# Decay inside chunks of 128, running state sums on VectorE, v scaled on ScalarE, output copies in free buffers, and another pace of weights

## The chip, the cores and the metric

The kernel runs on one core of one Trainium2 chip. The metric is the device time of one execution in microseconds (us). TensorE does the matmuls, VectorE, ScalarE and GpSimd the elementwise work, and SyncE (SP) issues all DMAs, in one order.

## What is computed

A retention layer, that is causal attention with a fixed decay per head and no softmax, feeds two networks with one hidden layer each.

```python
# q, k, v: (4, 8, 576, 64) float32; x: 2304 tokens x 512; w_in: 512 x 2048; w_out: 2048 x 512
scores = scale * np.matmul(q, k.transpose(0, 1, 3, 2))
gamma = 1.0 - 2.0 ** (-5.0 - np.arange(H, dtype=np.float32))
rel = pos[:, None] - pos[None, :]
Dmat = np.where(rel >= 0, gamma[:, None, None] ** rel[None, :, :], 0.0)
x = np.matmul(scores * Dmat, v)          # then (token, head * 64) rows
h = x @ w_in                             # first network
x = (np.maximum(h, 0.0) + alpha * np.minimum(h, 0.0)) @ w_out
h = x @ w_in2                            # second network
out = (h * (1.0 / (1.0 + np.exp(-1.702 * h)))) @ w_out2
```

All weights come as float64, and the kernel turns them into float32 itself.

## The kernel before

**Attention.** The work is 16 pairs, each two heads of one batch element (`PAIRS`). A sequence of 576 is cut into four chunks of 128 and a rest of 64. Per pair TensorE computes the scores inside each chunk (`a_scores`, tile `sc`), the state sums k^T v (`a_outer`, tile `st`), and the output from both (`a_values`, tile `av`). The state that chunk c reads is the sum over all earlier chunks; TensorE forms each of the four states from scratch, 1 + 2 + 3 + 4 products for each head. The decay is split into a factor on v (`vtab`) and one on the output (`otab`), both counted over the whole sequence from position 256. GpSimd scales v in place (`a_v`). VectorE masks the scores into SBUF (`a_evac`, tile `r`) and scales the output (`a_out`, into `xs`). ScalarE copies the states (`a_states`). At the start eight matmuls on a 34 KB table spread `otab` over the partitions (tile `tab`). The loop over i is a hand-made software pipeline: in step i TensorE does states and scores of pair i, then the output of pair i - 1; the loads (`ld`: q, k, v, 864 KB; `kn`: k once more, 256 KB) run three pairs ahead. Every engine works in the order in which the program issues.

**Weights.** A weight tile (`raw`, 512 KB, three buffers) is loaded, then one ScalarE operation (`w_abs`) and four on VectorE (`w_float`) make it float32 (`cv`, four buffers); a rounded high part (`w_hi`, ScalarE) and the rest (`w_lo`, a subtraction on VectorE) go into the tile `w`. The sixteen `w` slots serve in the attention as buffers of `ld`, `r` and `xs`. Times of all this are written by hand: `at(t, ...)` files an event, and `run_to(t)` issues what is due. In the first stage t counts pairs, later steps of the networks (`base` is the first). Second-network weights are converted early, stored (`w2_store`) and loaded again late (`w2_load`, two halves in one tile `w2f` in the buffers of `raw`).

**Networks.** Tokens lie in five chunks (512, the last, chunk 4, 256), x and the hidden values are split in two as the weights are, and three products of the parts make one. A step is one chunk and one of 16 blocks of hidden units: 12 matmuls into `h` (`mm1`), the activation, the split into `gs`, and two steps later 12 matmuls into four sums `acc` (`mm2`). `BLOCKS` orders the steps: chunks 0 and 1 first run with half of the hidden units, since the other weights are not there yet; their half sums go out to `pt` and come back as `part`. At the end of a block four copies `o` go out:

```python
o = mp.tile([128, 512], F32, tag="g2", name="o", bufs=3)[:, 0:N]
```

These three buffers serve the negative branch `g2` of the first activation too. A step with 512 tokens is 24 matmuls. The split of `gs` is on VectorE in the first 22 steps and on GpSimd after them.

## Time and profile before

| | |
|---|---|
| median of 3 runs (lowest to highest) | 912.92 us (911.67 to 915.03) |
| the profiled execution | 916.01 us, span of its profile 914.2 us |
| TensorE busy | 885.6 us, 97% of the span |
| VectorE, ScalarE, GpSimd busy | 404.8, 328.6, 189.8 us |
| mean granted clock of TensorE | 0.991 |

The span is what the profiler records from the first to the last instruction, and the execution's own time lies 1.8 us above it. A busy share is a mean over stages with different limits. A row of the timeline merges like instructions and gives start, length, engine, line, operation, tiles, count, and in brackets the idle time ahead of it with what ended it. PEld is TensorE's weight load, which runs beside the matmuls.

### The profile page before, as it was taken

The page shows a single profiled execution, that of the slowest core. Times are in us where ns is not written, and L with a number is a line of the kernel's source. Part 1 is how long each engine was busy: PE and PEld are TensorE (multiplying, and loading weights), DVE is VectorE, ACT ScalarE, POOL GpSimd, SP SyncE. Part 2 cuts the span into 40 slices and gives each one's busy share as a digit, 9 for nine tenths or more (in the row PEclk, how much of TensorE's full clock was granted, in tenths as well). Part 3 has the DMA queues.
Part 4 walks back from the last instruction along what each step waited for, and adds up shares of the span by engine and source line. Part 5 has one row for each costly group of instructions (what it writes and reads, how often), then busy time and mean ns, then how long its engine had stood idle before and what let it go on. Part 6 is the DMA issues. An engine that isn't in the chain of part 4 may idle for free.

```text
span 914.2 us, 13404 instructions
## 1 busy us (share of the span) xinstructions
PE 885.6 (97%) x5408; PEld 746.8 (82%) x5408; DVE 404.8 (44%) x625; ACT 328.6 (36%) x618; POOL 189.8 (21%) x173
## 2 busy tenths in 40 slices
...
GB/s 208 268 253 286 103 253 126 128 116 80 52 53 105 217 204 178 150 132 108 161 177 208 137 25 24 1 70 1 23 1 70 1 24 0 58 6 6 34 14 24
DMA packets 37086, 93.30 MB, mean 102 GB/s; under 512 B 4376, under 2 KB 9112, under 8 KB 37024
## 3 DMA queue, kind: packets, MB, share of 16 engines
...
## 4 chain that ended last, share of the span: by engine, by line
PE 67%; issue 15%; DVE 9%; POOL 4%; DMA 3%; ACT 2%; SPq 0%; POOLq 0%; DVEq 0%; ACTq 0%
PE acc L354 33%; PE h L304 33%; POOL gs L81 2%; DVE cv L115 2%; POOL ld L181 2%; DVE g L319 1%; DVE cv L119 1%; DVE cv L111 1%; DVE cv L108 1%; DVE w L81 1%; DVE gs L81 1%; DMA ld<-in_qkv_dram 1%; DMA pt<-o 1%; POOL r L222 1%; DMA out_dram<-o 1%
## 5 line engine op out<-in xcount | busy, mean ns | idle before, releaser
L354 PE MATMUL acc<-gs,w 128*128 128x512 f32 (+1 forms) x1920 | 426.1, 370 | 12.1 <-ACT o L78 3.7
L304 PE MATMUL h<-x,w 128*128 128x512 f32 (+1 forms) x1920 | 420.1, 368 | 0.7 <-DVE xs L248 0.7
L354 PEld LDWEIGHTS acc<-gs,w 128*128 128x128 f32 x1920 | 336.9, 189 | 78.0 <-POOL gs L81 6.2
L304 PEld LDWEIGHTS h<-x,w 128*128 128x128 f32 x1920 | 336.8, 189 | 61.2 <-DVE xs L248 0.9
L81 POOL TENSOR_TENSOR gs<-g,gs 128x512 fp32r<-128x512 f32 (+1 forms) x137 | 164.2, 1199 | 642.9 <-ACT gs L78 532.8
L324 DVE TENSOR_TENSOR g<-h,g 128x512 f32<-128x512 f32 (+1 forms) x80 | 51.0, 638 | 306.4 <-ACT g L323 306.4
L78 ACT ACTIVATE gs<-g 128x512 fp32r<-128x512 f32 (+1 forms) x160 | 94.2, 589 | 104.0 <-DVE g L319 56.2
L323 ACT ACTIVATE g<-h 128x512 f32<-128x512 f32 (+1 forms) x80 | 44.3, 554 | 218.6 <-PE h L304 218.6
L319 DVE SCALAR_TENSOR_TENSOR g<-g,nalpha_sb,g 128x512 f32<-128x512 f32 (+1 forms) x80 | 56.2, 703 | 113.9 <-ACT g L318 113.9
L317 ACT ACTIVATE g<-h 128x512 f32<-128x512 f32 (+1 forms) x80 | 43.6, 545 | 77.8 <-PE h L304 77.7
L115 DVE SCALAR_TENSOR_TENSOR cv<-raw,cv 128x512 int32<-128x512 int32 x64 | 62.8, 981 | 2.2
L103 ACT ACTIVATE cv<-raw 128x512 f32<-128x512 f32 x64 | 42.5, 666 | 35.4 <-DMA raw<-in_w1i_dram 9.9
L119 DVE SCALAR_TENSOR_TENSOR cv<-raw,cv 128x512 int32<-128x512 int32 x64 | 45.3, 707 | 2.2
L318 ACT ACTIVATE g<-h 128x512 f32<-128x512 f32 (+1 forms) x80 | 43.8, 548 | 2.4 <-DMA x<-o 2.4
L78 ACT ACTIVATE w<-cv 128x512 fp32r<-128x512 f32 x32 | 20.2, 631 | 53.6 <-DVE cv L119 53.6
L81 DVE TENSOR_TENSOR x<-xf,x 128x512 fp32r<-128x512 f32 (+1 forms) x32 | 29.9, 934 | 19.9 <-ACT x L78 19.9
L108 DVE TENSOR_SCALAR cv<-cv 128x512 f32<-128x512 f32 x64 | 31.0, 484 | 2.2 <-ACT cv L103 2.1
L214 DVE TENSOR_TENSOR r<-sc,mask_sb 128x1024 f32<-128x1024 f32 x16 | 19.5, 1220 | 26.5 <-PE sc L186 24.7
L186 PEld LDWEIGHTS st<-ld,kn 128*64 128x64 f32 x640 | 21.3, 144 | 11.9 <-POOL ld L181 11.1
L186 PE MATMUL st<-ld,kn 128*64 128x64 f32 x640 | 23.3, 231 | 7.8 <-POOL ld L181 7.7
L111 DVE TENSOR_SCALAR cv<-cv 128x512 int32<-128x512 int32 x64 | 28.2, 441 | 2.2
L78 ACT ACTIVATE o<-acc 128x512 f32<-128x512 f32 (+1 forms) x20 | 11.1, 555 | 44.5 <-DMA out_dram<-o 14.9
...
## 6 DMA issues: line engine op xcount, KB each, us to landing
ld<-in_qkv_dram SPq DMA_DIRECT2D x15, 864.0 KB, 5.0
...
w<-cv SPq DMA_DIRECT2D x32, 256.0 KB, 2.5
...
kn<-in_kn_dram SPq DMA_DIRECT2D x16, 256.0 KB, 5.7
```

Of the source, the lines that this page charges most:

```text
L78: return nc.scalar.activation(out=out, in_=in_, func=ACTF.Copy)
L81: return eng.tensor_tensor(out=out, in0=a, in1=b.bitcast(F32), op=ALU.subtract)
L115: nc.vector.scalar_tensor_tensor(out=g, in0=raw[:, :, 1], scalar=-(1 << 30), in1=g, op0=ALU.bitwise_and, op1=ALU.bitwise_or,)
L119: nc.vector.scalar_tensor_tensor(out=g, in0=raw[:, :, 0], scalar=29, in1=g, op0=ALU.logical_shift_right, op1=ALU.bitwise_or,)
L186: nc.tensor.matmul(out=out, lhsT=lhsT, rhs=rhs, start=start, stop=stop, skip_group_check=True)
L304: nc.tensor.matmul(out=t, lhsT=w[:, cw, k * 128:k * 128 + 128], rhs=x[:, cx], start=(i == 0), stop=(i == 3 * NK - 1),)
L317: nc.scalar.activation(out=g, in_=t, func=ACTF.Relu)
L318: nc.scalar.activation(out=g2, in_=t, func=ACTF.Relu, scale=-1.0)
L319: nc.vector.scalar_tensor_tensor(out=g, in0=g2, scalar=nalpha_sb[:, m:m + 1], in1=g, op0=ALU.mult, op1=ALU.add)
L323: nc.scalar.activation(out=g, in_=t, func=ACTF.Sigmoid, scale=1.702)
L324: nc.vector.tensor_tensor(out=g, in0=t, in1=g, op=ALU.mult)
L354: nc.tensor.matmul(out=acc[0][d], lhsT=w[:, cw, d * 128:d * 128 + 128], rhs=g[:, cx], start=(j == m0 and i == 0), stop=(j == m1 - 1 and i ...
```

## The change

The decay is counted within each chunk of 128. A chunk's own sum k^T v then stands alone, so `a_outer` issues four products for each head. ScalarE scales the states by the decay of 128 positions while it copies them, and VectorE adds the running sum with three operations of 64 columns (`scalar_tensor_tensor`, line 228 after the change). The table of v shrinks to four columns, and ScalarE scales v with three operations, issued before the step's evacuation, no longer at the step's end. The table of the output comes ready from DRAM, 160 KB for each of the first four pairs, so the eight table matmuls and their copies go. PSUM is dealt out anew: `st` has one buffer for two, `av` three for two. In the attention GpSimd does the subtractions of x (`xa_split`) and of seven weights, of which there were eight. The copies `o` of a half block go into the slot of the sixteenth `w` tile (`os`), the others into the buffers of x that the block has read. The reload of second-network weights uses two tiles. The events have other times, and chunk 2 runs before chunk 4.

```diff
...
 BLOCKS = [(0, c, h * HALF, h * HALF + HALF) for h in range(2) for c in (0, 1)]
-BLOCKS += [(0, c, 0, NM) for c in (4, 2, 3)]
+BLOCKS += [(0, c, 0, NM) for c in (2, 4, 3)]
 BLOCKS += [(1, c, 0, NM) for c in range(5)]
...
 
-    vtab_sb = att.tile([128, NP, 9, 1], F32, name="vtab_sb")
+    vtab_sb = att.tile([128, NP, 4], F32, name="vtab_sb")
     mask_sb = att.tile([128, 1, 1, 192], F32, name="mask_sb")
-    rows_sb = wp.tile([8, NP * 128 + S], F32, tag=f"w{TMP['xs'][-1]}", name="rows_sb")
-    otab_sb = att.tile([128, NP, S], F32, name="otab_sb")
+    otab_sb = att.tile([128, NP, 320], F32, name="otab_sb")
     alpha_sb = const.tile([128, NM], F32, name="alpha_sb")
...
 
-    def w_lo(key):
+    def w_lo(key, eng=nc.vector):
         l, c, m = key
         wt[key] = wt[l, m][:, c]
-        sub(nc.vector, wt[key][:, 1], cvs.pop(key), wt[key][:, 0])
-
-    def w_first(t, key, src, gap):
-        at(t - 3.2 * gap, w_load, key, src, key[2])
+        sub(eng, wt[key][:, 1], cvs.pop(key), wt[key][:, 0])
+
+    def w_first(t, key, src, eng):
+        at(t - 1.5, w_load, key, src, key[2])
         at(t, w_abs, key)
-        at(t + gap, w_float, key)
-        at(t + 2 * gap, w_hi, key)
-        at(t + 3 * gap, w_lo, key)
+        at(t + 0.5, w_float, key)
+        at(t + 1.0, w_hi, key)
+        at(t + 1.5, w_lo, key, eng)
 
...
     def w2_load(m):
-        f = cvp.tile([128, 2, DM], F32, tag="raw", name="w2f", bufs=3)
-        nc.sync.dma_start(out=f, in_=w2s[m])
-        for c in range(2):
-            cvs[2, c, m] = f[:, c]
+        for c, (tag, bufs) in enumerate((("raw", 3), ("cv", 4))):
+            cvs[2, c, m] = cvp.tile([128, DM], F32, tag=tag, name="w2f", bufs=bufs)
+            nc.sync.dma_start(out=cvs[2, c, m], in_=w2s[m][:, c])
 
...
             nc.sync.dma_start(out=t[:, 1152:1728], in_=qkv[b, p, :, 1152:1728])
-            nc.sync.dma_start(out=rows_sb, in_=otab)
         else:
...
         nc.sync.dma_start(out=n, in_=kn[b, p])
+        if i < NP:
+            nc.sync.dma_start(out=otab_sb[:, i], in_=otab[:, i])
         q = [t[:, j * 128:j * 128 + 128] for j in (0, 1, 4, 5)] + [t[:, 768:832]]
...
 
+    def scale(out, in_, by):
+        nc.scalar.activation(out=out, in_=in_, func=ACTF.Copy, scale=by)
+
     def a_v(i):
         v, p = ld[i][2], PAIRS[i][1]
-        nc.gpsimd.tensor_tensor(
-            out=v, in0=v, in1=vtab_sb[:, p].to_broadcast([128, 9, 64]), op=ALU.mult
-        )
+        for e in range(2):
+            scale(v[:, e:8:2], v[:, e:8:2], vtab_sb[:, p, e:e + 1])
+        scale(v[:, 8], v[:, 8], vtab_sb[:, p, 2:3])
 
...
         if i not in s_t:
-            s_t[i] = aps.tile([128, 512], F32, tag="st", name="st", bufs=2)
-        for c in range(1, 5):
-            for j in range(c):
-                for e, o in enumerate(halves):
-                    mm(s_t[i][o, c * 64:c * 64 + 64], n[:, j, o], v[:, 2 * j + e], c == 1 and i > 0, j == c - 1)
+            s_t[i] = aps.tile([128, 512], F32, tag="st", name="st")
+        for j in range(4):
+            for e, o in enumerate(halves):
+                mm(s_t[i][o, j * 64 + 64:j * 64 + 128], n[:, j, o], v[:, 2 * j + e], j == 0 and i > 0, True)
 
...
         if i not in s_t:
-            s_t[i] = aps.tile([128, 512], F32, tag="st", name="st", bufs=2)
+            s_t[i] = aps.tile([128, 512], F32, tag="st", name="st")
         for o in halves:
...
     def a_states(i):
-        copy(r_t[i][1], s_t.pop(i)[:, 0:320])
+        s, g = r_t[i][1], vtab_sb[:, PAIRS[i][1], 3:4]
+        scale(s, s_t.pop(i)[:, 0:320], g)
         nc.gpsimd.tensor_tensor(
-            out=r_t[i][1][:, 0:64], in0=r_t[i][1][:, 0:64], in1=mask_sb[:, 0, 0, 128:192], op=ALU.mult
-        )
+            out=s[:, 0:64], in0=s[:, 0:64], in1=mask_sb[:, 0, 0, 128:192], op=ALU.mult
+        )
+        for c in range(128, 320, 64):
+            nc.vector.scalar_tensor_tensor(
+                out=s[:, c:c + 64], in0=s[:, c - 64:c], scalar=g, in1=s[:, c:c + 64],
+                op0=ALU.mult, op1=ALU.add,
+            )
 
...
         r, s = r_t.pop(i)
-        t = [aps.tile([128, 512], F32, tag=f"av{h}", name="av") for h in range(2)]
+        t = [aps.tile([128, 512], F32, tag="av", name="av", bufs=3) for h in range(2)]
         av_t[i] = t
...
             nc.vector.tensor_tensor(
-                out=xs[:, s0:s1], in0=t[h][:, 0:s1 - s0], in1=otab_sb[:, p, s0:s1], op=ALU.mult
+                out=xs[:, s0:s1], in0=t[h][:, 0:s1 - s0], in1=otab_sb[:, p, 0:s1 - s0], op=ALU.mult
             )
...
         copy(x[:, 0], f)
-        sub(nc.vector, x[:, 1], f, x[:, 0])
+        sub(nc.gpsimd, x[:, 1], f, x[:, 0])
 
...
         if layer == 0:
-            g2 = mp.tile([128, 512], F32, tag="g2", name="g2", bufs=3)[:, 0:N]
+            g2 = mp.tile([128, 512], F32, tag="g2", name="g2", bufs=2)[:, 0:N]
             nc.scalar.activation(out=g, in_=t, func=ACTF.Relu)
...
         if m == m1 - 1:
+            if m1 < NM:
+                os = wp.tile([128, NK, 512], F32, tag=f"w{NM - 1}", name="os")
             for d in range(NK):
-                o = mp.tile([128, 512], F32, tag="g2", name="o", bufs=3)[:, 0:N]
+                if m1 < NM:
+                    o = os[:, d]
+                else:
+                    o = homes[layer, c].tile([128, 512], F32, tag=f"x{d}", name="o")[:, 0:N]
                 if m0:
...
         src = (w1i, w1o)[key[1]]
-        if n < 8:
-            w_first(3 + 1.6 * n, key, src, 0.25)
+        if n < 7:
+            t = 2.5 + 1.8 * n
         elif n < 16:
-            w_first(base - 1 + 0.68 * (n - 8), key, src, 0.5)
+            t = base - 1.2 + 0.66 * (n - 7)
         else:
-            w_first(base + 5 + 0.85 * (n - 16), key, src, 0.5)
+            t = base + 5.5 + 0.95 * (n - 16)
+        w_first(t, key, src, nc.gpsimd if n < 7 else nc.vector)
     for i in range(n_a):
...
         nc.vector.memset(wz, 0.0)
-        wps = aps.tile([128, 512], F32, tag="av0", name="wps")
+        wps = aps.tile([128, 512], F32, tag="av", name="wps", bufs=3)
         for i in range(8):
...
                 a_outer(i)
+            if i + 1 < n_a:
+                a_v(i + 1)
             run_to(i)
...
                 a_states(i)
-            if i == 0:
-                for p in range(NP):
-                    for h, (s0, s1) in enumerate(((0, 256), (256, S))):
-                        t = aps.tile([128, 512], F32, tag=f"av{h}", name="tab")[:, 0:s1 - s0]
-                        r0 = NP * 128
-                        mm(t, rows_sb[:, p * 128:p * 128 + 128], rows_sb[:, r0 + s0:r0 + s1], True, True)
-                        copy(otab_sb[:, p, s0:s1], t)
             run_to(i + 0.25)
...
                 a_load(i + 3)
-            if i + 1 < n_a:
-                a_v(i + 1)
             run_to(i + 0.75)
...
             steps += [(layer, c, m, m0, m1) for m in range(m0, m1)]
-        n_x = 2
-        for layer, c, m0, _ in BLOCKS[4:]:
+        homes = {(0, c): xp[c] for c in range(2)}
+        for n, (layer, c, m0, _) in enumerate(BLOCKS[4:]):
+            homes[layer, c] = xp[n % 2]
             for k in range(NK):
-                t = starts[layer, c, m0] - 7 + 1.5 * k
+                t = starts[layer, c, m0] - 6 + 1.3 * k
                 at(t - 2, x_load, layer, c, k)
-                at(t, x_split, layer, c, k, xp[n_x % 2])
-            n_x += 1
+                at(t, x_split, layer, c, k, xp[n % 2])
         for c in range(2):
             for d in range(NK):
-                at(starts[0, c, HALF] + 5 + 0.3 * d, part_load, c, d)
-        t2 = starts[0, 4, 0] + 3
+                at(starts[0, c, HALF] + 7.5, part_load, c, d)
         n1 = starts[1, 0, 0]
...
             for c, src in ((0, w2i), (1, w2o)):
-                key = (2, c, m)
-                t = t2 + 1.25 * (2 * m + c)
+                key, n = (2, c, m), 2 * m + c
+                if n < 5:
+                    t = base + 26.2 + 0.9 * n
+                elif n < 21:
+                    t = base + 33.5 + 0.85 * (n - 5)
+                else:
+                    t = base + 47.5 + 1.45 * (n - 21)
                 at(t - 1.6, w_load, key, src, m)
...
     p = np.arange(128)
-    j = np.stack([p - 256, p - 128, p, p + 128])
-    vt = (gam[:, None, None] ** (-j[None].astype(np.float64))).reshape(NP, 2, 4, 128)
-    tail = (gam[:, None] ** -(256.0 + np.arange(64))).reshape(NP, 1, 128)
-    vt = np.concatenate([vt.transpose(0, 2, 1, 3).reshape(NP, 8, 128), tail], axis=1)
-    d["vtab"] = vt.transpose(2, 0, 1).astype(np.float32)
-    i = np.concatenate([np.arange(256) - 256, np.arange(320)])
-    ot = gam[:, None] ** i[None, :].astype(np.float64) / float(D) ** 0.5
-    rows = np.concatenate([np.repeat(np.eye(H), 64, axis=1), ot], axis=1)
-    d["otab"] = rows.astype(np.float32)
+    decay = lambda n: (gam[:, None] ** n.astype(np.float64)).reshape(NP, 2, -1)
+    half = lambda t: np.repeat(t, 64, axis=1)
+    key = decay(-p)
+    tail = decay(-128 - p[:64]).reshape(NP, 128)
+    vt = np.stack([key[:, 0], key[:, 1], tail, half(decay(np.array([128])))[..., 0]], axis=2)
+    d["vtab"] = vt.transpose(1, 0, 2).astype(np.float32)
+    ot = decay(np.arange(320) % 128) / float(D) ** 0.5
+    d["otab"] = half(ot).transpose(1, 0, 2).astype(np.float32)
     tri = p[None, :] >= p[:, None]
     return {n: np.ascontiguousarray(d[n]) for n in _INS}
```

TensorE's order within one pair (st: states, sc: scores, av: output) was this:

```order
L186 MATMUL st<-ld,kn 64x64 x20
L186 MATMUL sc<-ld 128x128 x8
L186 MATMUL st<-ld 64x64 x2
L186 MATMUL av<-ld,r 64x128 x6
L186 MATMUL av<-ld,r 64x64 x2
```

and is now:

```order
L188 MATMUL st<-ld,kn 64x64 x8
L188 MATMUL sc<-ld 128x128 x8
L188 MATMUL st<-ld 64x64 x2
L188 MATMUL av<-ld,r 64x128 x6
L188 MATMUL av<-ld,r 64x64 x2
```

Only the first row has become shorter; nothing has changed its place. On VectorE, where a pair of the second batch element and a weight conversion meet (xs: output, cv: weight), the order was:

```order
L214 TENSOR_TENSOR r<-sc,mask_sb 128x1024
L108 TENSOR_SCALAR cv<-cv 128x512
L111 TENSOR_SCALAR cv<-cv 128x512
L115 SCALAR_TENSOR_TENSOR cv<-raw,cv 128x512
L119 SCALAR_TENSOR_TENSOR cv<-raw,cv 128x512
L81 TENSOR_TENSOR x<-xs,x 128x448
L248 TENSOR_TENSOR xs<-av,otab_sb 128x256
L248 TENSOR_TENSOR xs<-av,otab_sb 128x320
L81 TENSOR_TENSOR w<-cv,w 128x512
```

and is now:

```order
L215 TENSOR_TENSOR r<-sc,mask_sb 128x1024
L228 SCALAR_TENSOR_TENSOR r<-r,vtab_sb 128x64 x3
L107 TENSOR_SCALAR cv<-cv 128x512
L110 TENSOR_SCALAR cv<-cv 128x512
L114 SCALAR_TENSOR_TENSOR cv<-raw,cv 128x512
L118 SCALAR_TENSOR_TENSOR cv<-raw,cv 128x512
L255 TENSOR_TENSOR xs<-av,otab_sb 128x256
L255 TENSOR_TENSOR xs<-av,otab_sb 128x320
```

The two subtractions are gone, and the three multiply-adds stand behind the evacuation. On ScalarE, at the same place, the order was:

```order
L78 ACTIVATE r<-st 128x320
L103 ACTIVATE cv<-raw 128x512
L78 ACTIVATE x<-xs 128x448
L78 ACTIVATE w<-cv 128x512
L78 ACTIVATE r<-st 128x320
L78 ACTIVATE x<-xs 128x448
```

and is now:

```order
L179 ACTIVATE r<-st,vtab_sb 128x320
L102 ACTIVATE cv<-raw 128x512
L77 ACTIVATE x<-xs 128x448
L179 ACTIVATE ld<-ld,vtab_sb 128x4x64 x2
L179 ACTIVATE ld<-ld,vtab_sb 128x64
L179 ACTIVATE r<-st,vtab_sb 128x320
L77 ACTIVATE w<-cv 128x512
L77 ACTIVATE x<-xs 128x448
```

Three scalings of v (tile `ld`) now stand ahead of each copy of the states (`r<-st`).

## Rows read from the trace of the kernel before

**Rows 1.** Busy time of each engine by stretch, then PEclk (granted clock), DMA share, GB/s.

```profile
23.02:94.79 71.77, 62.91 (x1248) 55.88 (x1248) 54.58 (x87) 19.69 (x40) 21.02 (x26) 0.98 0.76 267
102.82:914.20 811.38, 795.67 (x3840) 669.30 (x3840) 339.47 (x521) 300.95 (x563) 164.20 (x137) 1.00 0.26 85
...
62.00:66.00 4.00, 2.33 (x32) 1.99 (x34) 2.83 (x5) 1.42 (x3) 1.54 (x2) 0.93 0.96 376
66.00:68.40 2.40, 2.40 (x28) 2.28 (x26) 1.92 (x3) 1.15 (x2) 0.00 (x0) 0.50 0.06 24
```

**Rows 2.** Timeline of the attention, TensorE: state matmuls, and the networks' first matmuls.

```profile
16.16 2.40 PE L186 MATMUL st<-ld,kn 128*64 128x64 f32 x40
...
23.02 1.39 PE L186 MATMUL st<-ld,kn 128*64 128x64 f32 x40
...
27.87 1.39 PE L186 MATMUL st<-ld,kn 128*64 128x64 f32 x40 [0.20 <-POOL ld L181]
...
94.79 1.39 PE L186 MATMUL st<-ld,kn 128*64 128x64 f32 x40 [0.19 <-POOL ld L181]
...
102.82 8.46 PE L304 MATMUL h<-x,w 128*128 128x512 f32 x36 [0.67 <-DVE xs L248]
```

**Rows 3.** TensorE's waits after 103 us: total us, times, longest us.

```profile
PE acc L354 <- ACT o L78: 3.7, 3, 2.2
...
PE acc L354 <- DVE o L363: 2.0, 1, 2.0
```

**Rows 4.** Timeline, TensorE and ScalarE, near the end of the first network.

```profile
465.23 2.88 PE L304 MATMUL h<-x,w 128*128 128x512 f32 x12
...
492.97 1.15 ACT L78 ACTIVATE w<-w2f 128x512 fp32r<-128x512 f32 x2 [3.54 <-DMA w2f<-w]
...
501.19 2.88 PE L354 MATMUL acc<-gs,w 128*128 128x512 f32 x12
```

**Rows 5.** Instructions grouped by line and shape: busy us, mean ns, idle before.

```profile
L81 POOL TENSOR_TENSOR gs<-g,gs 128x512 fp32r<-128x512 f32 x106 | 139.7, 1317 | 564.1 <-ACT gs L78 481.9 <-PE acc L354 82.2
...
L319 DVE SCALAR_TENSOR_TENSOR g<-g,nalpha_sb,g 128x512 f32<-128x512 f32 x64 | 48.5, 758 | 100.6 <-ACT g L318 100.6
...
L214 DVE TENSOR_TENSOR r<-sc,mask_sb 128x1024 f32<-128x1024 f32 x16 | 19.5, 1220 | 26.5 <-PE sc L186 24.7 <-PE st L186 1.9
...
L319 DVE SCALAR_TENSOR_TENSOR g<-g,nalpha_sb,g 128x256 f32<-128x256 f32 x16 | 7.7, 480 | 13.3 <-ACT g L318 13.3
...
L78 ACT ACTIVATE r<-st 128x320 f32<-128x320 f32 x16 | 6.9, 433 | 23.7 <-PE st L186 23.6
```

**Rows 6.** Timeline, VectorE: both output products; a conversion's first operation, and its subtraction.

```profile
27.82 0.81 DVE L248 TENSOR_TENSOR xs<-av,otab_sb 128x256 f32<-128x256 f32 x2
...
107.78 0.42 DVE L108 TENSOR_SCALAR cv<-cv 128x512 f32<-128x512 f32 x1
...
110.03 0.68 DVE L81 TENSOR_TENSOR w<-cv,w 128x512 fp32r<-128x512 f32 x1
```

**Rows 7.** Timeline, GpSimd and VectorE at 78 us.

```profile
78.25 1.15 POOL L181 TENSOR_TENSOR ld<-ld,vtab_sb 128x576 f32<-128x576 f32 x1
78.34 1.33 DVE L108 TENSOR_SCALAR cv<-cv 128x512 f32<-128x512 f32 x1
```

**Rows 8.** Timeline, GpSimd: the second pair's v.

```profile
10.61 1.15 POOL L181 TENSOR_TENSOR ld<-ld,vtab_sb 128x576 f32<-128x576 f32 x1 [0.53 <-DMA ld<-in_qkv_dram]
```

**Rows 9.** Timeline, TensorE and ScalarE, at the end of the first half block.

```profile
152.47 2.88 PE L304 MATMUL h<-x,w 128*128 128x512 f32 x12
...
157.40 4.58 PE L354 MATMUL acc<-gs,w 128*128 128x512 f32 x12 [2.04 <-DVE o L367]
...
159.38 0.60 ACT L78 ACTIVATE o<-acc 128x512 f32<-128x512 f32 x1 [4.71 <-DMA pt<-o]
...
161.81 2.91 PE L304 MATMUL h<-x,w 128*128 128x512 f32 x12
```

**Rows 10.** DMA issues: KB each, median us from issue to landing.

```profile
ld<-in_qkv_dram SPq DMA_DIRECT2D x15, 864.0 KB, 5.0
```

4 lines of the change are left out of this document (2 added, 2 removed).

## Prediction

> **What bounds the kernel now.** I read the stretches first: they set TensorE's busy time against the span, stage by stage. From the third pair's state matmuls to the last pair's, 23.02 to 94.79 us, TensorE is busy 62.91 of 71.77 us, and VectorE is busy 54.58 [rows 1]. In the stage of the two networks TensorE is busy 795.67 of 811.38 us [rows 1]. That leaves two things to win: work of TensorE and waits in the first 103 us, and about 16 us of gaps behind it. TensorE's timeline gives the pace of the first stage. A pair that meets little resistance takes 27.87 - 23.02 = 4.85 us, 0.20 of it a wait for GpSimd's scaling of v; the 13 pairs between the third and the last take 71.77 / 13 = 5.52 us each [rows 1, 2]. The pairs that take longer carry a weight conversion on VectorE. The waits of the second stage then say what the gaps are: copies of finished sums (o) that stand still [rows 3], and one stretch around 480 us in which weights of the second network come late [rows 4].
>
> **Attention, TensorE.** A pair's state sums go from 20 matmuls to 8. The profile counts each as two, and 40 of them take 1.39 us [rows 2], so 24 fewer save 0.83 us. The wait of 0.20 us is for v, which ScalarE will scale one step earlier in the order. The floor of a pair becomes 4.85 - 0.20 - 0.83 = 3.82 us.
>
> **Attention, VectorE.** It keeps the evacuation, 1.22 us [rows 5], and the two output products, 0.81 us [rows 6]. It gains three multiply-adds of 64 columns. No row shows these. The same operation takes 758 ns at 512 columns and 480 ns at 256 [rows 5], 1.09 ns a column, which leads to about 270 ns at 64 as my estimate; the bounds are nothing and 480 ns each. I take 0.27, the end of that line, so 0.8 us a pair (0 to 1.44). It loses the subtractions of x and of the attention-time weights to GpSimd. A conversion without its subtraction, four operations, is 110.03 - 107.78 = 2.25 us [rows 6]. Seven of 16 pairs carry one: 1.22 + 0.81 + 0.81 + 2.25 = 5.1 us. The other nine need 2.8 and stand at TensorE's 3.82. If no slack passes from one pair to the next, the mean is (7 x 5.1 + 9 x 3.82) / 16 = 4.4 us; if all of it passes, 3.85. I take 4.4, because before, too, conversions lengthen the pair in which they stand.
>
> **Attention, GpSimd.** Its scaling of v goes; eight subtractions of 448 or 512 columns and seven of weights come, at 1.32 us each [rows 5], 20 us in all (four of 64 columns are small). What one costs VectorE is the open price. A VectorE operation of 0.42 us [rows 6] that began 0.09 us after a GpSimd operation took 1.33, ending 0.27 us behind it [rows 7]. So the bounds are nothing and the whole 20 us (1.24 us a pair). I take a tenth, 0.13 a pair: the evacuation and the output products read PSUM, and the three multiply-adds are short. The Trainium skill (SBUF — State Buffer, "Who interferes with whom") says that a VectorE instruction with two SBUF inputs and a GpSimd instruction that reads SBUF shut each other out for the whole instruction. The rows agree, 1.33 us for 0.42; by that rule the multiply-adds and conversions are exposed to each new subtraction, and all of them meeting one would give the third rival's time. My pace is 4.4 + 0.1 = 4.5 us a pair, between 3.8 and 5.6.
>
> **Attention, the engines that cover.** ScalarE was busy 19.69 us in 13 pairs, 1.5 each [rows 1]. Its three scalings of v cost at most three times the 433 ns of its 320-column copy [rows 5], 1.3 us: 2.8 of 4.5, so I cost them at nothing. What stands behind them matters more: the copy of the states is queued behind the next pair's scaling, which waits for that pair's load. State sums have one PSUM buffer now, so the next pair's state matmuls and the multiply-adds wait for that copy. If this cover fails, the price is the second rival's.
>
> **Attention, start.** The eight table matmuls go; before, the second pair's states began at 16.16 and the third's at 23.02 [rows 2]. The second load came at 10.61 [rows 8]. Ahead of it now lies a table of 160 KB for 34 KB, 0.3 us at 376 GB/s [rows 1]. Add 1.3 for v and 0.43 for the states' copy: the second pair begins near 12.7, 3.4 us earlier. Its states need 24 of 40 matmuls less of the 2.40 us taken there [rows 2], 1.4 more, unless TensorE is granted its high clock later than before. I take 4.1 (3.4 to 4.9). The last stretch, 94.79 to 102.82 [rows 2], I leave: it loses 0.83 of matmuls and gains a conversion ahead of the last product. Sum: 4.1 + 13 x (5.52 - 4.5) = 17.4 us.
>
> **Networks, copies of sums.** At the end of the first half block TensorE needs 161.81 - 152.47 = 9.34 us for two groups that take 5.44 elsewhere (2.72 each): 3.9 us lost, 2.04 as a wait and the rest because the next 12 matmuls take 4.58 us and not 2.88 [rows 9]. The cause stands on ScalarE: its copy into o waits 4.71 us for a store, since three buffers serve o and the negative branch [rows 9]. The other block ends cost 3.7 us in three waits and 2.0 in one [rows 3]. The new buffers (the slot of the sixteenth weight tile, later x's own) have four places each, and their earlier readers are two steps back. So these 3.9 + 3.7 + 2.0 = 9.6 us go; the lower bound is nothing, if the places come free late.
>
> **Networks, pace of weights.** From 465.23 to 501.19 TensorE does 11 groups, 29.9 us of work in 35.96: 6.0 us lost, while ScalarE waits for second-network weights, 3.54 us in one case, ahead of the copy that feeds TensorE [rows 4]. Their reloads share the SP queue and the buffers with the last conversions. Now all conversions are issued before the first reload, so I count 6.0 gained (bounds 0 and 6.0). Against it: nine first-network weights instead of eight fall into the first steps, where VectorE is full; the extra one is 2.25 us and a subtraction of about 0.7, of which I take 0.5 as a stall (0 to 2.9). The order of chunks 2 and 4 moves the short steps away from the early conversions and under the late ones: nothing, plus or minus 1.5. Sum: 9.6 + 6.0 - 0.5 = 15.1 us.
>
> **The sum.** 17.4 + 15.1 = 32.5 us. The profiled execution took 916.0 us (span 914.2), 0.3% above the median of 912.9; from that median, 880.
>
> **Rivals.** *TensorE paces every pair* at 3.82 us: slack does pass on, as VectorE's mean of 3.85 allows. Gain 4.9 + 22.1 + 15.6: 870 us. *Loads pace the pairs*: 1.38 MB a pair with its share of weights at the stretch's 267 GB/s [rows 1] is 5.2 us, and ScalarE stands in front of the states' copy until they land (5.0 us from issue [rows 10]). For it: the loads have less lead now. Against: 376 GB/s was reached at a share of 0.96 [rows 1], 3.7 us a pair. Gain 4.1 + 4.2 + 15.1: 889.5 us. *GpSimd shuts VectorE out*: 5.6 us a pair; gain 4.1 - 1.0 + 15.1: 895 us. *The copies still wait* because the new places are held by stores or readers: without the 9.6, 890 us. *Slower*: TensorE stays at its lower clock, 1.2 GHz, through the attention. From 66.0 to 68.4 us it was granted 0.50, after four microseconds in which it was busy for 2.33 [rows 1]. A pair then takes 7.64 us, 3.14 above my pace; from 32.5 / 3.14 = 10.4 pairs on the kernel is slower, and 13 give 921 us. Sparser matmuls speak for it; that TensorE held a clock of 0.98 over the 13 pairs at 88% busy [rows 1] speaks against, since 3.82 of 4.5 is 85%. The Trainium skill (TensorE: Matmul & The Clock Gate, "Part 1: The HAM clock gate") makes the low state the default and activity what lifts it; the stretch at 66 us agrees.
>
> **How the numbers follow.** My forecast has 0.66 and a range of its own of 868 to 889. TensorE-paced 0.09, loads 0.10, GpSimd 0.08, waiting copies 0.04, slower 0.03. 867 to 893 holds the first, the fast one, the loads and the waiting copies, less the ends. About 0.5%, 4.6 us, is what a measurement can tell from no change. Only the clock ends slower: 0.03. Within 0.5% needs two of the bad cases together: 0.02. Faster: 0.95.
>
> **What would show it.** The stage of the networks begins near 85 us; the state matmuls stand about 4.5 us apart, wider where a conversion stands; the 64-column multiply-adds take near 0.27 us. No wait for o at a block end, and none of ScalarE for w2f near the end of the first network. I would be wrong if ScalarE's scaling waits long for loads, if multiply-adds run to GpSimd's end, or if the granted clock falls in the attention.

## The result, and the profile after

The changed kernel takes 881.41 us, median of 4 runs (880.08 to 883.86), against 913.71 us of the kernel before, also 4 runs: a ratio of 0.965, with an interval of 0.962 to 0.968. The forecast was 880. The profiled execution took 883.86 us, its span 882.1, which is 32.1 below the span of before. The stretches show where these 32.1 us lie.

```profile
19.60:80.70 61.10, 53.26 (x940) 48.02 (x938) 57.19 (x103) 32.22 (x75) 22.96 (x32) 0.94 0.82 297
87.39:882.10 794.71, 790.01 (x3842) 668.89 (x3840) 346.49 (x529) 304.78 (x565) 164.60 (x137) 1.00 0.27 87
```

These answer to the first two of [rows 1]: the 13 pairs between the third and the last, and the networks. VectorE is now busy 57.19 of 61.10 us, so it has taken TensorE's place as the busiest engine of the attention. In the networks all that is left above TensorE's own 790 us is 4.7 us. TensorE's timeline gives the borders:

```profile
13.00 1.12 PE L188 MATMUL st<-ld,kn 128*64 128x64 f32 x16 [2.68 <-ACT r L179]
...
19.60 0.63 PE L188 MATMUL st<-ld,kn 128*64 128x64 f32 x16
...
23.33 0.64 PE L188 MATMUL st<-ld,kn 128*64 128x64 f32 x16
...
80.70 0.63 PE L188 MATMUL st<-ld,kn 128*64 128x64 f32 x16
...
87.39 8.50 PE L311 MATMUL h<-x,w 128*128 128x512 f32 x36
```

Against [rows 1, 2] the start of the third pair gained 23.02 - 19.60 = 3.4 us, the 13 pairs 71.77 - 61.10 = 10.7 (5.52 to 4.70 a pair), the end of the attention 8.03 - 6.69 = 1.3, and the networks 811.38 - 794.71 = 16.7. An unhindered pair takes 23.33 - 19.60 = 3.73 us; the longest of the 13 takes 7.06. Behind the attention TensorE waits for no copy o any more; [rows 3] have become these two:

```profile
PE acc L361 <- ACT gs L77: 1.0, 1, 1.0
PE acc L361 <- POOL gs L80: 0.4, 2, 0.3
```

The new operations, by line and shape (busy us, mean ns, idle before):

```profile
L228 DVE SCALAR_TENSOR_TENSOR r<-r,vtab_sb 128x64 f32<-128x64 f32 x48 | 22.1, 460 | 7.1 <-ACT r L179 5.8
...
L179 ACT ACTIVATE ld<-ld,vtab_sb 128x256 f32<-128x256 f32 x32 | 14.5, 499 | 21.9 <-DMA ld<-in_qkv_dram 21.8
...
L80 POOL TENSOR_TENSOR w<-cv,w 128x512 fp32r<-128x512 f32 x7 | 9.0, 1285 | 1.8 <-ACT w L77 1.8
```

A multiply-add takes 460 ns in the mean, not 270. VectorE's timeline shows both kinds, and GpSimd's what ran beside them:

```profile
39.80 0.92 DVE L228 SCALAR_TENSOR_TENSOR r<-r,vtab_sb 128x64 f32<-128x64 f32 x3
40.63 0.81 DVE L255 TENSOR_TENSOR xs<-av,otab_sb 128x256 f32<-128x256 f32 x2
41.36 1.24 DVE L107 TENSOR_SCALAR cv<-cv 128x512 f32<-128x512 f32 x1
...
45.60 2.58 DVE L228 SCALAR_TENSOR_TENSOR r<-r,vtab_sb 128x64 f32<-128x64 f32 x3
```

```profile
41.19 1.13 POOL L80 TENSOR_TENSOR x<-xs,x 128x448 fp32r<-128x448 f32 x1 [1.20 <-ACT x L77]
...
45.76 1.13 POOL L80 TENSOR_TENSOR x<-xs,x 128x448 fp32r<-128x448 f32 x1 [1.75 <-ACT x L77]
46.84 1.26 POOL L80 TENSOR_TENSOR w<-cv,w 128x512 fp32r<-128x512 f32 x1
```

At 39.80 three multiply-adds take 0.92 us with nothing large on GpSimd. At 45.60 the same three take 2.58 us, beside GpSimd's two subtractions from 45.76 to 48.1. Last, what answers to [rows 10]: a load of q, k and v now lands 7.0 us after its issue, no longer 5.0.

```profile
ld<-in_qkv_dram SPq DMA_DIRECT2D x15, 864.0 KB, 7.0
```

### The profile page after: what moved, and what is told of

It reads as the page before. It is cut to its first block, busy times and chain, and to the rows that moved or that the text cites. A ratio compares the mean times of both kernels' runs of the same rounds, so it can differ in the third digit from the quotient of the medians.

```text
span 882.1 us, 12646 instructions
## 1 busy us (share of the span) xinstructions
PE 863.1 (98%) x5008; PEld 734.4 (83%) x5008; DVE 414.8 (47%) x654; ACT 345.5 (39%) x658; POOL 189.8 (22%) x176
## 4 chain that ended last, share of the span: by engine, by line
PE 86%; DVE 8%; issue 2%; ACT 1%; DMA 1%; POOL 0%; SPq 0%; POOLq 0%; ACTq 0%
PE acc L361 41%; PE h L311 40%; PE av L188 2%; DVE cv L114 1%; DVE r L228 1%; PE sc L188 1%; DVE cv L110 1%; DMA ld<-in_qkv_dram 1%; DVE r L215 1%; PE st L188 1%; DVE cv L107 1%; DVE xs L255 1%; DVE g L326 1%; DVE gs L80 1%; DVE w L80 1%
## 5 line engine op out<-in xcount | busy, mean ns | idle before, releaser
L361 PE MATMUL acc<-gs,w 128*128 128x512 f32 (+1 forms) x1920 | 420.9, 368 | 1.5 <-ACT gs L77 1.0
L114 DVE SCALAR_TENSOR_TENSOR cv<-raw,cv 128x512 int32<-128x512 int32 x64 | 66.7, 1042 | 2.2
L118 DVE SCALAR_TENSOR_TENSOR cv<-raw,cv 128x512 int32<-128x512 int32 x64 | 44.8, 699 | 2.2
L179 ACT ACTIVATE ld<-ld,vtab_sb 128x256 f32<-128x256 f32 (+1 forms) x48 | 18.3, 444 | 21.9 <-DMA ld<-in_qkv_dram 21.8
L228 DVE SCALAR_TENSOR_TENSOR r<-r,vtab_sb 128x64 f32<-128x64 f32 x48 | 22.1, 460 | 7.1 <-ACT r L179 5.8
L188 PE MATMUL av<-ld,r 64*64 64x128 f32 (+1 forms) x256 | 17.9, 273 | 6.5 <-DVE xs L255 6.4
```

The lines of the kernel that those rows point to most:

```text
L114: nc.vector.scalar_tensor_tensor(out=g, in0=raw[:, :, 1], scalar=-(1 << 30), in1=g, op0=ALU.bitwise_and, op1=ALU.bitwise_or,)
L118: nc.vector.scalar_tensor_tensor(out=g, in0=raw[:, :, 0], scalar=29, in1=g, op0=ALU.logical_shift_right, op1=ALU.bitwise_or,)
L188: nc.tensor.matmul(out=out, lhsT=lhsT, rhs=rhs, start=start, stop=stop, skip_group_check=True)
L361: nc.tensor.matmul(out=acc[0][d], lhsT=w[:, cw, d * 128:d * 128 + 128], rhs=g[:, cx], start=(j == m0 and i == 0), stop=(j == m1 - 1 and i ...
```

## Experiments

Each kernel is the changed one with one edit, unless said otherwise. To read them by stage, this table has, from the profiled execution of each, when the networks begin, the mean of the 13 pairs between the third and the last, and the length of the networks. Experiments 1, 2, 7 and 8 shared a chip with runs of before at 915.74 us, 3, 4, 9 and 10 at 915.25, 5, 6 and 11 at 915.33, and 12 at 914.40.

| kernel | median us | ratio to before | networks begin | us a pair | networks |
|---|---|---|---|---|---|
| before | 913.71 | 1 | 102.82 | 5.52 | 811.4 |
| changed | 881.41 | 0.965 (0.962 to 0.968) | 87.39 | 4.70 | 794.7 |
| 1: sums on TensorE | 881.50 | 0.962 (0.957 to 0.967) | 84.70 | 4.59 | 794.2 |
| 2: subtractions on VectorE | 882.97 | 0.964 (0.958 to 0.970) | 85.60 | 4.61 | 795.1 |
| 3: both | 881.68 | 0.963 (0.960 to 0.966) | 86.34 | 4.58 | 794.5 |
| 4: v on GpSimd, late | 894.62 | 0.978 (0.975 to 0.981) | 100.19 | 5.80 | 793.9 |
| 5: v on GpSimd, early | 889.95 | 0.973 (0.968 to 0.978) | 93.19 | 5.21 | 794.1 |
| 6: v on ScalarE, late | 881.65 | 0.964 (0.959 to 0.968) | 86.48 | 4.73 | 793.8 |
| 7: old buffers of o | 883.28 | 0.964 (0.959 to 0.969) | 85.21 | | 796.3 |
| 8: old pace, second network | 889.15 | 0.971 (0.966 to 0.976) | 86.48 | | 800.6 |
| 9: old pace and buffers | 893.92 | 0.976 (0.973 to 0.980) | 84.64 | | 807.8 |
| 10: old pace, new buffers | 890.59 | 0.974 (0.971 to 0.976) | 86.24 | | 802.1 |
| 11: sums added from PSUM | 879.13 | 0.962 (0.956 to 0.968) | 82.01 | 4.34 | 794.6 |
| 12: the same, conversions in halves | 879.47 | 0.962 (0.960 to 0.964) | 83.73 | 4.35 | 794.0 |

The changed kernel and experiments 7 to 10 have the same attention but for a shift in the first weights' times, and their networks begin between 84.64 and 87.39 us. Differences below 3 us in that column are therefore not read as effects. Networks that are those of the changed kernel (experiments 1 to 6, 11 and 12) take 793.8 to 795.1 us, each in one profiled execution, so the last column is good to about 1 us. The medians come from chips on which the kernel before took 0.7 to 2.0 us more than the 913.71 that belong to 881.41; from one chip to another the ratios are the fairer comparison.

**Theories.** The prediction put the attention's gain on fewer state matmuls and on VectorE's lighter load, and that of the networks on new buffers for o (9.6 us) and on the weights' pace (6.0). The rival for the attention: it hangs on the edit that was costed at nothing, v scaled by ScalarE. The rival for the networks: the pace alone removes the waits for o. A further rival for the attention was not run: the weights converted there are seven instead of eight, and they are loaded and converted at other times.

### 1. State sums on TensorE again, without multiply-adds

```diff
-        for j in range(4):
-            for e, o in enumerate(halves):
-                mm(s_t[i][o, j * 64 + 64:j * 64 + 128], n[:, j, o], v[:, 2 * j + e], j == 0 and i > 0, True)
+        for c in range(1, 5):
+            for j in range(c):
+                for e, o in enumerate(halves):
+                    mm(s_t[i][o, c * 64:c * 64 + 64], n[:, j, o], v[:, 2 * j + e], c == 1 and i > 0, j == c - 1)
...
-        for c in range(128, 320, 64):
-            nc.vector.scalar_tensor_tensor(
...
```

> The changed kernel with the state sums on TensorE again: 20 state matmuls a pair instead of eight, and no multiply-adds on VectorE. Left out is the decay between chunks in these sums, so the values differ; the amount of work is that of the kernel before. My theory, TensorE paces the pairs without a conversion and VectorE the others: the pairs of 3.73 us go to about 4.55, the longer ones get shorter by about the multiply-adds, and the networks begin at 90 to 93 us, total 884 to 887 us. Rival, TensorE paces all pairs: 0.83 us on each of 16, networks near 100 us, total near 894. Rival, VectorE paces all: networks near 80 us, total near 873.

Measured: 881.50 us, no slower than the changed kernel; neither the theory's 884 to 887 us nor a rival's time. Its stretch of 13 pairs:

```profile
18.46:78.07 59.61, 58.58 (x1253) 54.08 (x1249) 44.59 (x68) 31.82 (x75) 23.21 (x30) 1.00 0.87 304
```

TensorE is busy 58.58 of 59.61 us, 5.3 more than with the change, and VectorE 12.6 less. TensorE now paces the pairs, where VectorE does in the changed kernel. The load has only changed engines: what TensorE saves by the smaller sums, the multiply-adds take back on VectorE.

### 2. The subtractions back on VectorE

```diff
-        sub(nc.gpsimd, x[:, 1], f, x[:, 0])
+        sub(nc.vector, x[:, 1], f, x[:, 0])
...
-        w_first(t, key, src, nc.gpsimd if n < 7 else nc.vector)
+        w_first(t, key, src, nc.vector)
```

> The changed kernel with the 15 large and four small subtractions of the attention back on VectorE. My theory is that VectorE's own work with the time for which GpSimd holds it sets the pace of the longer pairs: VectorE gets about 11 us of subtractions (12 of x and seven of weights, 0.23 to 0.7 us each) and is freed of about 9 us (48 multiply-adds at 0.46 us on average instead of 0.27). So the networks should begin within 2 us of the 87.4 us of the changed kernel, and the multiply-adds should all take under 0.3 us. Rival, GpSimd's hold alone costs the time: the networks begin 3 us or more earlier, near 84 us. Rival, moving the subtractions was the gain: they begin 5 us or more later.

Measured: 882.97 us and 4.61 us a pair, the same time. The multiply-adds fall to 289 ns in the mean, since GpSimd no longer holds them up, and VectorE spends what it saves so on the subtractions. Moving them neither gains nor loses.

### 3. Both of these undone together

> The changed kernel with both parts undone that made no difference one at a time: 20 state matmuls a pair without multiply-adds (leaves out the decay between chunks), and the subtractions of x and of the attention's weights on VectorE. Theory (the gain of the attention lies elsewhere: tables, time and engine of v, seven conversions at another pace): 881 to 884 us, pairs of 4.6 to 4.8 us. Rival (each of the two alone makes the slack that the pairs need, so only undoing both shows it): pairs of 5.2 us or more, 888 to 892 us.

```profile
20.17:79.70 59.53, 58.78 (x1253) 54.53 (x1249) 49.49 (x85) 32.25 (x76) 4.86 (x12) 1.00 0.85 305
```

```profile
20.17 1.33 PE L188 MATMUL st<-ld,kn 128*64 128x64 f32 x40
...
24.60 1.33 PE L188 MATMUL st<-ld,kn 128*64 128x64 f32 x40
```

Measured: 881.68 us, 4.58 us a pair; the theory held. Here TensorE has the 20 state matmuls of before and VectorE the subtractions of before, and yet the 13 pairs take 59.53 us where before took 71.77 [rows 1]. The gain needs neither of the two edits on which the prediction had built its pace. An unhindered pair takes 24.60 - 20.17 = 4.43 us here and took 4.85 before, with the same matmuls. Of these 0.42 us the trace of before showed 0.20 as a wait for v.

### 4. v scaled by GpSimd at the step's end, as before

```diff
-        for e in range(2):
-            scale(v[:, e:8:2], v[:, e:8:2], vtab_sb[:, p, e:e + 1])
-        scale(v[:, 8], v[:, 8], vtab_sb[:, p, 2:3])
+        by = vtab_sb[:, p, 4:13].rearrange("p (n o) -> p n o", o=1).to_broadcast([128, 9, 64])
+        nc.gpsimd.tensor_tensor(out=v, in0=v, in1=by, op=ALU.mult)
...
-            if i + 1 < n_a:
-                a_v(i + 1)
             run_to(i)
...
                 a_load(i + 3)
+            if i + 1 < n_a:
+                a_v(i + 1)
             run_to(i + 0.75)
```

> The changed kernel with v scaled by GpSimd at the end of the step, as before. Theory (v on ScalarE and issued earlier is a part of the gain in the attention): TensorE's states wait for GpSimd again, the multiply-adds meet one more GpSimd operation a pair; the 13 pairs go from 4.7 to about 5.1 us each, 885 to 888 us. Rival (ScalarE's 21.8 us of waits for loads hold up the copies of the states, so that taking v off ScalarE helps): 4.4 us a pair, 876 to 879 us. Neither matters: 880 to 883 us.

Measured: 894.62 us, 13.2 above the changed kernel (0.978 of before against 0.965) and more than any theory had said; the networks begin at 100.19 us. This one edit takes back 12.8 of the 15.4 us that the attention had gained. GpSimd's timeline, then TensorE's:

```profile
27.82 0.32 POOL L80 TENSOR_TENSOR x<-xs,x 128x64 fp32r<-128x64 f32 x1 [1.44 <-ACT x L77]
28.09 1.17 POOL L184 TENSOR_TENSOR ld<-ld,vtab_sb 128x576 f32<-128x576 f32 x1
```

```profile
29.32 0.69 PE L187 MATMUL st<-ld,kn 128*64 128x64 f32 x16 [2.48 <-POOL ld L184]
```

The scaling of v begins the moment that a 64-column subtraction of x lets it. GpSimd had waited 1.44 us for that subtraction's input, a copy of ScalarE. TensorE's states, queued behind all this, waited 2.48 us, and 18.1 us over 13 pairs. An engine works in the order of issue: v of the next pair stood behind work of this pair that waits for two other engines.

### 5. v scaled by GpSimd, but issued early

The edit of experiment 4 without the move to the step's end.

> The changed kernel with v scaled by GpSimd, but issued where the change issues it, ahead of the step's evacuation. Theory (the place decides: at the step's end the scaling stood behind GpSimd's mask product of the same step, which waits for ScalarE's copy of the states, which waits for TensorE's states, and the next pair's states wait for the scaling, so that a pair lasted as long as this loop): issued early it is outside the loop, pairs of 4.7 to 4.9 us, 881 to 885 us. Rival (the engine decides: one more GpSimd operation a pair, and each shuts VectorE out): pairs of 5.2 us or more, 889 to 895 us, as when it stood at the step's end.

Measured: 889.95 us, 4.7 below experiment 4 and 8.5 above the changed kernel. The rival's range held (889 to 895 us, pairs of 5.2 or more), but the place has its part. Out of the queue's end, v no longer makes TensorE wait; what it does now stands in VectorE's group of multiply-adds and in TensorE's waits, both over the 13 pairs:

```profile
L227 DVE SCALAR_TENSOR_TENSOR r<-r,vtab_sb 128x64 f32<-128x64 f32 x37 | 24.6, 664 | 0.9
```

```profile
PE av L187 <- DVE xs L254: 11.6, 7, 3.1
```

With one more GpSimd operation a pair the multiply-adds of this stretch take 664 ns, where the changed kernel's take 493; VectorE's output products come late, and TensorE waits 11.6 us for them. VectorE is busy 7.8 us more than in the changed kernel, 6.9 of them in the multiply-adds, which the kernel before did not have.

### 6. v scaled by ScalarE, but at the step's end

> The changed kernel with v scaled by ScalarE, but issued at the step's end, as before. Theory of the place: the scaling stands behind the copy of the states and the splits on ScalarE, TensorE's states wait for it, pairs of 5.1 to 5.6 us, 887 to 894 us. Rival (the engine): 880 to 884 us, pairs of 4.7 us.

Measured: 881.65 us. On ScalarE the place costs nothing, so the theory of the place fell for it. TensorE waits 4.2 us for the scaled v, and the pairs are no longer for it. In the changed kernel, then, with the multiply-adds on VectorE and the subtractions on GpSimd, v must not be on GpSimd. What v there costs without these two, as in the kernel before, no run shows.

### 7. Copies o in the three shared buffers again

```diff
-            g2 = mp.tile([128, 512], F32, tag="g2", name="g2", bufs=2)[:, 0:N]
+            g2 = mp.tile([128, 512], F32, tag="g2", name="g2", bufs=3)[:, 0:N]
...
-                if m1 < NM:
-                    o = os[:, d]
-                else:
-                    o = homes[layer, c].tile([128, 512], F32, tag=f"x{d}", name="o")[:, 0:N]
+                o = mp.tile([128, 512], F32, tag="g2", name="o", bufs=3)[:, 0:N]
```

> The changed kernel with the output copies in the three buffers that they share with the negative branch, as before. The term of the prediction: 9.6 us come back, less what the first long step after a half block hides now, so 888 to 891 us, with waits of TensorE for the copies at the two ends of the first half blocks, 2 us each, and the lower granted clock behind the first. Rival, the other pace of weights had taken these waits away by itself: 881 to 883 us.

Measured: 883.28 us; the networks take 796.3 us, 1.6 more, where 7 to 9.6 were expected. In the whole time nothing of it is clear of noise (0.964 of before against 0.965). TensorE waits for o at the end of the first half block alone, 1.0 and 0.3 us.

### 8. The old pace and reload of the second network's weights

```diff
-                if n < 5:
-                    t = base + 26.2 + 0.9 * n
-                elif n < 21:
-                    t = base + 33.5 + 0.85 * (n - 5)
-                else:
-                    t = base + 47.5 + 1.45 * (n - 21)
+                t = base + 35 + 1.25 * n
...
-        for c, (tag, bufs) in enumerate((("raw", 3), ("cv", 4))):
-            cvs[2, c, m] = cvp.tile([128, DM], F32, tag=tag, name="w2f", bufs=bufs)
-            nc.sync.dma_start(out=cvs[2, c, m], in_=w2s[m][:, c])
+        f = cvp.tile([128, 2, DM], F32, tag="raw", name="w2f", bufs=3)
+        nc.sync.dma_start(out=f, in_=w2s[m])
```

> The changed kernel with the conversions of the second network's weights at their times of before (one each 1.25 steps from the 35th step) and the reload in one tile. The term of the prediction: about 6 us come back, 887 us, and ScalarE waits for reloaded weights in front of the copies that feed TensorE, in the last eight steps of the first network. Rival, those waits came with the old order of chunks or from the output copies: 881 to 883 us.

Measured: 889.15 us; the networks take 800.6 us, 5.9 more. TensorE's waits in them:

```profile
PE acc L362 <- ACT gs L77: 4.1, 3, 1.7
PE acc L362 <- POOL gs L80: 2.0, 4, 0.6
```

Of the first line 1.0 us lies at the end of the first half block, as in the changed kernel; the other two waits, 1.4 and 1.7 us, begin near 443 and 468 us. There ScalarE waits for reloaded weights, as in [rows 4], up to 5.5 us in one case.

### 9 and 10. The network part undone, with the old and with the new buffers of o

Both have the old pace of both networks' weights, the old reload and the old order of chunks; experiment 9 has the edit of experiment 7 too.

```diff
-BLOCKS += [(0, c, 0, NM) for c in (2, 4, 3)]
+BLOCKS += [(0, c, 0, NM) for c in (4, 2, 3)]
...
-            t = base - 1.2 + 0.66 * (n - 7)
+            t = base - 1 + 0.68 * (n - 8)
...
-            t = base + 5.5 + 0.95 * (n - 16)
+            t = base + 5 + 0.85 * (n - 16)
...
-                at(starts[0, c, HALF] + 7.5, part_load, c, d)
+                at(starts[0, c, HALF] + 5 + 0.3 * d, part_load, c, d)
```

> The attention of the changed kernel with the networks' part undone: copies o in the three g2 buffers, reload in one tile, the old pace of both networks' weights and the old chunk order (the splits of x keep their new times). Theory (the two stages add up): the networks lose what they gained, 16.7 us, so 898 us (894 to 901), their stage takes about 811 us again, TensorE waits near 2 us for o at the end of the first half block, and the wait for second-network weights near the end of the first network is back. Rival (a part of that gain came from a lighter end of the attention): 888 to 892 us, and the first half block ends without a wait for o.

> As the kernel with the networks' part undone, but with the new buffers of o. Theory of the prediction (the buffers alone are worth 9.6 us): 9 to 10 us below that kernel, near 888 us. Rival (the pace and the order of the weights decide when the stores go out, and the buffers are worth the 1.6 us that they were worth under the new pace): within 3 us of that kernel, 895 to 900 us. Third (buffers and pace each remove the same waits, either is enough): near 888 us too, and then the small loss under the new pace was this substitution.

Measured: 893.92 us with the old buffers, just below the 894 to 901 of the theory, and 890.59 with the new, 3.3 less: more than the 888 of two theories and less than the 895 of the rival. Together with the changed kernel and experiment 7 this makes a square of the networks' lengths: old pace 807.8 (old buffers) and 802.1 (new), new pace 796.3 and 794.7. The buffers are worth 5.7 us under the old pace and 1.6 under the new; the pace is worth 11.5 us with the old buffers and 7.4 with the new. By the medians the buffers are worth 3.3 under the old pace. So each takes over a part of the other's work, as the third theory had it, but the pace is the larger. A part of the pace's share is clock: near the end of the first network experiments 9 and 10 each have ten matmuls that take 4.14 and 4.15 us, where experiment 8 has them in 2.56 to 2.60. At the end of the first half block one sees how, in TensorE's timelines of experiments 9 and 10:

```profile
139.96 2.32 PE L362 MATMUL acc<-gs,w 128*128 128x512 f32 x9 [2.08 <-DVE o L375]
```

```profile
141.57 3.00 PE L362 MATMUL acc<-gs,w 128*128 128x512 f32 x12 [2.09 <-ACT gs L77]
```

With new buffers the wait for o is gone and one as long for gs stands in its place: VectorE is full there, busy 4.83 and 4.90 us of the two stretches of 5 us from 135 to 145, and ScalarE's rounding of weights waits for it. The new pace halves that one, to 1.0 us.

Experiment 9 gave 807.8 us in the networks and not the 811.4 of before. A part of the missing 3.6 us is TensorE's clock. In windows of 5 us before has

```profile
155.00:160.00 5.00, 2.96 (x9) 2.06 (x8) 3.41 (x6) 0.62 (x2) 0.00 (x0) 0.76 0.48 188
160.00:165.00 5.00, 5.00 (x21) 4.08 (x20) 3.30 (x6) 3.53 (x7) 0.00 (x0) 0.90 0.51 162
```

and experiment 9, at the same place of the program,

```profile
135.00:140.00 5.00, 2.92 (x14) 2.14 (x12) 4.90 (x10) 2.09 (x4) 0.00 (x0) 1.00 0.32 105
140.00:145.00 5.00, 4.64 (x19) 3.51 (x20) 1.80 (x4) 3.02 (x6) 0.00 (x0) 1.00 0.68 236
```

The waits at this place are alike (2.04 and 2.08 us), but before was then granted 0.76 and 0.90 of the clock, which is 5 x (0.24 + 0.10) = 1.7 us, and experiment 9 the whole. The rest lies among what experiment 9 had not undone (the times of x's splits, the weights of the attention), and in its trace the waits for o at later block ends are shorter; which edit does it stays open.

### 11. The multiply-adds read the chunk's sums from PSUM

```diff
-        scale(s, s_t.pop(i)[:, 0:320], g)
+        t = s_t.pop(i)
+        scale(s[:, 0:128], t[:, 0:128], g)
...
-                out=s[:, c:c + 64], in0=s[:, c - 64:c], scalar=g, in1=s[:, c:c + 64],
-                op0=ALU.mult, op1=ALU.add,
+                out=s[:, c:c + 64], in0=s[:, c - 64:c], scalar=1.0 if c == 128 else g,
+                in1=t[:, c:c + 64], op0=ALU.mult, op1=ALU.add,
...
+    def a_rescale(i):
+        s = r_t[i][1][:, 128:320]
+        scale(s, s, vtab_sb[:, PAIRS[i][1], 3:4])
...
+            if i:
+                a_rescale(i - 1)
```

> The changed kernel with the multiply-adds reading the chunk's sums from PSUM, so that one of their two inputs lies in SBUF; ScalarE copies only the first 128 columns before them and rescales the other 192 a step later; st gets two PSUM buffers and av two. Theory (VectorE paces the pairs, 57.19 of 61.10 us busy, and 8.4 us of it is multiply-adds held up by GpSimd): they fall to about 0.3 us each, pairs of 4.2 to 4.4 us, 875 to 878 us. Rival (loads or TensorE's output waits take over): multiply-adds are short, but pairs stay at 4.6 us or more, 880 to 883 us. If the multiply-adds still take 0.46 us each, the second SBUF input is not what holds them up.

Measured: 879.13 us, 1 us above the forecast's range, and 4.34 us a pair, within it. The 32 multiply-adds that multiply by the decay take 281 ns in the mean, and the 16 others, the first of each pair, 216. VectorE's timeline, then GpSimd's:

```profile
43.95 0.60 DVE L229 SCALAR_TENSOR_TENSOR r<-r,vtab_sb,st 128x64 f32<-128x64 f32 x2
...
47.73 1.16 DVE L107 TENSOR_SCALAR cv<-cv 128x512 f32<-128x512 f32 x1
```

```profile
43.86 1.13 POOL L80 TENSOR_TENSOR x<-xs,x 128x448 fp32r<-128x448 f32 x1 [1.03 <-ACT x L77]
...
47.48 1.13 POOL L80 TENSOR_TENSOR x<-xs,x 128x448 fp32r<-128x448 f32 x1
```

At 43.95 two multiply-adds run at full speed in the middle of a GpSimd subtraction. At 47.73 a conversion's first operation, whose only tensor input lies in SBUF, is still held: 1.16 us for 0.42. So it is the second SBUF input that held the multiply-adds. The Trainium skill (SBUF — State Buffer, "Who interferes with whom") says both: two SBUF inputs collide with GpSimd's reads, and an operation with one such input does so only in VectorE's two-port mode, which its tensor_scalar can enter. The trace agrees with each: 281 ns, and 1.16 us. The shorter pair is worth what the whole edit is worth, with a shorter copy on ScalarE and two buffers of st; the multiply-adds alone were not separated.

### 12. The conversions of the attention in halves

Experiment 11 with this:

```diff
-            at(t + 0.5, w_float, key)
-        at(t + 1.0, w_hi, key)
-        at(t + 1.5, w_lo, key, eng)
+        late = 0.9 if eng is nc.gpsimd else 0
+        if late:
+            at(t + 0.5, w_float, key, 0)
+            at(t + 0.5 + late, w_float, key, 1)
...
+        at(t + 1.0 + late, w_hi, key)
+        at(t + 1.5 + late, w_lo, key, eng)
```

> The kernel with the multiply-adds from PSUM, and each of the seven weight conversions of the attention split over two pairs: the two operations that clamp and shift at the old time, the two that join the bits 0.9 pairs later, with the rounding and the subtraction behind them. Theory (VectorE's load of single pairs paces them: 2.9 us without a conversion, 5.1 with one, against 3.73 us of TensorE, and little slack is passed on): every pair now has at most 4.3 us on VectorE, the 13 pairs go from 4.34 to about 4.0 us each, and the time is 874 to 877 us. Rival (loads, or waits inside a pair, pace them): pairs of 4.3 us or more, 878 to 881 us.

Measured: 879.47 us, median of 5 runs, and 4.35 us a pair, where about 4.0 were expected. The theory fell: spreading the conversions did not bring the pairs nearer to TensorE's 3.73 us. The stretch of 20 to 44 us shows what else is full:

```profile
20.00:44.00 24.00, 23.13 (x426) 20.59 (x421) 21.72 (x45) 16.33 (x42) 12.86 (x18) 1.00 0.96 347
```

The 16 DMA engines move 347 GB/s at a share of 0.96, and before reached 376 GB/s at the same share [rows 1]. That the loads are the next bound is argued from this row, not shown; no run took loads away. The same row leaves little room for it: TensorE is itself busy 23.13 of the 24 us. The pairs behind 44 us are the longer ones, and there TensorE was granted 0.50 of its clock from 47 to 50 us.

Experiments 11 and 12 are the fastest kernels here, 2 us below the changed one. Their intervals, 0.956 to 0.968 and 0.960 to 0.964, overlap its own, so that they are faster than it is likely and not settled.

## Why the prediction was right, and where it was not

The total was right, 881.4 for 880, and the sums by stage were near: 15.4 us gained in the attention for 17.4, 16.7 in the networks for 15.1. Inside them two terms were put on the wrong cause, and that the sums still came out is in part luck.

**Attention, TensorE and VectorE.** The floor of a pair was right, 3.73 us for 3.82, but by two errors that cancel: the smaller sums saved 4.43 - 3.73 = 0.70 us and not 0.83, and what went with the wait for v was 0.42 and not 0.20 (experiment 3). That VectorE paces the changed kernel's longer pairs was right too. (The mean of its load with all slack passed on is (7 x 5.1 + 9 x 2.8) / 16 = 3.81 us, not 3.85; nothing hangs on that.) But "24 fewer save 0.83 us" and "it loses the subtractions" do not make the pace. Undone one at a time and together they left 4.6 us a pair (experiments 1 to 3). What sets all three apart from before must lie among the edits that the prediction costed at little or nothing. The step that failed is the one that costed v at 0.20 us, from a single pair. The trace of before had more, in TensorE's waits from 23 to 95 us:

```profile
PE st L186 <- POOL ld L181: 5.8, 10, 1.4
PE av L186 <- DVE xs L248: 3.0, 3, 1.7
```

Ten waits for GpSimd's v, 5.8 us, nearly twice what stood behind VectorE. By the order of issue the scaling was the last of a ring: states, their copy on ScalarE, the mask product on GpSimd, v on GpSimd, the next states. The list of waits over the whole stretch shows these ten at once; the one pair that I had read shows a mild one. In the changed kernel, where GpSimd has the subtractions too, the ring is slower still (experiment 4, 5.80 us a pair).

That v alone explains the 12.2 us between the 13 pairs of before and those of experiment 3 is not shown. In the long waits something else stands in the ring, as in this one, from the timelines of ScalarE, GpSimd and TensorE of before:

```profile
30.62 0.67 ACT L103 ACTIVATE cv<-raw 128x512 f32<-128x512 f32 x1 [4.17 <-DMA raw<-in_w1i_dram]
...
31.71 0.43 ACT L78 ACTIVATE r<-st 128x320 f32<-128x320 f32 x1
...
32.68 1.15 POOL L181 TENSOR_TENSOR ld<-ld,vtab_sb 128x576 f32<-128x576 f32 x1
...
33.88 1.39 PE L186 MATMUL st<-ld,kn 128*64 128x64 f32 x40 [1.35 <-POOL ld L181]
```

The copy of the states stood behind a weight's first operation, which waited 4.17 us for its load. (So this pair, 6.01 us, was long without a conversion on VectorE.) The change also loads these weights earlier, and ScalarE's waits for them, before and in the 13 pairs of the changed kernel, are:

```profile
ACT cv L103 <- DMA raw<-in_w1i_dram: 9.9, 3, 4.2
...
ACT cv L103 <- DMA raw<-in_w1o_dram: 7.5, 3, 3.9
```

```profile
ACT cv L102 <- DMA raw<-in_w1i_dram: 0.6, 2, 0.4
```

No run gave the weights of the attention their old times, nor put v on GpSimd with the subtractions on VectorE. So v off GpSimd is needed by the changed kernel, the smaller sums and the moved subtractions are worth nothing measurable by themselves, and how the gain over before divides between v and the weights' times stays open.

**Attention, GpSimd and the multiply-adds.** 0.27 us was right for an undisturbed one (0.92 us for three, with the gaps between them), and the tenth taken for collisions was too little. The mean of 460 ns lies 175 above the median of the 48, 285 ns; that is 8.4 us in all and 0.5 us a pair, where 0.13 was taken. The rival "GpSimd shuts VectorE out" was thus half true: the collisions came, but the pace came out at 4.70 us for 4.5, not at 5.6, and without them it was no better (experiment 2). The row that the prediction took to agree with the rule for two SBUF inputs, 1.33 us for 0.42, is an operation with one tensor input; what bears on that rule is experiment 11.

**Attention, loads and start.** ScalarE waited 21.8 us for loads ahead of its scaling of v, as the second rival said, but the states' copy behind it came late for TensorE only twice, 2.7 us at the second pair and 1.7 in the 13 pairs. The start gained 3.4 us for 4.1, at the lower bound: the second pair came at 13.00 us, 0.3 late, and TensorE was granted 0.52 of its clock from 9.0 to 19.6 us. The end gained 1.3 us for nothing.

**Networks, copies of sums.** This term, 9.6 us for the buffers, is mis-attributed. The waits did go, but the buffers alone are worth 1.6 us under the new pace and 3.3 to 5.7 under the old. The step that failed is "the cause stands on ScalarE", its copy into an occupied buffer: it took the place where the wait ends for its cause. Given a free buffer, TensorE waits 2.09 us for gs at the same block end (experiment 10). Part of the 3.9 us there was a fall of the clock, which not every wait of that length brings.

**Networks, pace of weights.** 6.0 us for the second network was right, 5.9 measured (experiment 8). The whole of the new pace and order is worth 7.4 to 11.5 us, where the prediction had 5.5. One term of the networks was too large and the other too small by about as much, and so their sum was near.

**The clock.** The slower rival did not come. TensorE was granted 0.50 of its clock from 50 to 53 and from 74 to 77 us, after stretches of 3 us in which it was busy for 1.43 and 1.24, and its mean in the 13 pairs was 0.94. Experiment 6, with all the same work and a clock of 1.00 there, took 4.73 us a pair, and experiments 1 and 3, also with 1.00, were no faster than experiment 2 with 0.97: the falls made no measurable difference to the time. The Trainium skill (TensorE: Matmul & The Clock Gate, "Part 1: The HAM clock gate") ties the level to activity. The trace agrees, as far as each fall followed a stretch in which TensorE was less busy.
